# Seven products in place of eight for the gates of the last eight chunks, GpSimd's port in the plan, and new ranks

## The chip, the cores and the metric

One Trainium2 chip, one of its cores. The metric is the time of one execution in microseconds of device time; of several executions the median is given. The profile is of one execution.

## The reference, cut to what matters

Eight sequences of 576 tokens with eight heads go through random-feature attention, and the attended rows, 4,608 tokens of 512 numbers, through a bilinear feed-forward network:

```python
q_p, k_p = (phi(q_s), phi(k_s))            # 128 features a head: exp(x @ omega.T - |x|^2/2 - max)
kv = np.einsum('bhsm,bhsd->bhmd', k_p, v)
num = np.einsum('bhsm,bhmd->bhsd', q_p, kv)
den = np.einsum('bhsm,bhm->bhs', q_p, np.sum(k_p, axis=2))[..., None] + 1e-06
x = num / den                              # to 4608 x 512, heads side by side
a = x @ w1                                 # 512 -> 1024
b = x @ w2                                 # 512 -> 1024
out = ((a * b) @ w3) @ w_out               # 1024 -> 1024 -> 512
```

## The kernel before

The tokens are cut into 36 chunks of 128. Operands of most matmuls are float32 values split into two float16 halves, the value rounded and what is left of it; a product takes three passes (`PASSES`: high by high, high by low, low by high). The weights come as float64 words and are put together at the start; w3 and w_out are multiplied once into one matrix W.

For each chunk, k's features (`k_chunk`: projection `kpj`, maximum, exponential, split) meet v in `kv_batch` when a sequence is complete; q's features (`q_chunk`) are turned by DMA transposes; `q_attend` multiplies them with kv (`nu`), divides, scales by a power of two, splits the result into `xhl` and turns it by a DMA transpose on SP's queue into `xT`, which has three buffers of two chunks each.

`gate` (L1076 to L1124) takes chunks one by one up to chunk 3 and then in pairs. It forms a and b for all 1,024 hidden columns: per pair 8 blocks of hidden columns x 2 (a and b) x 4 blocks of the contraction x 3 passes, with the weights stationary and 256 columns of tokens moving (L1096). ScalarE copies a out of PSUM (L1108), VectorE multiplies b onto it (L1110), GpSimd splits the product into the two halves of `h` (L1116, L1118). `project_out` multiplies h by W, 24 matmuls of 512 columns a chunk (L1137); ScalarE scales the result (L1146) and SP's queue stores it.

No order is written out by hand. Each step is given to `Plan` by `op()` with the engines that could do it and a planned cost on each (`ways`), what it reads and writes, the buffers that it takes, whether it needs the port that VectorE and GpSimd share in the plan (`port`), and a rank. `Plan.order()` plays the program through with these costs: whenever an engine is free it begins the ready step of lowest rank whose buffers are free, and a step that needs the port begins only when no other holds it. The order so found is emitted, and each engine runs its instructions in that order. While TensorE would be idle up to a planned time the plan puts in matmuls with no use (`warm`, L434). A rank is a base (`base(c)`, 15.1 a chunk, less a lead for k and q) plus a number from the table `SHIFT`.

`hi()` (L444 to L447) writes the first half of a split with a per-partition factor; the plan may give it to ScalarE or to GpSimd, with GpSimd's cost `HI_POOL = 0.9` and no claim on the port. `split_raw` does this for q and k (`hlq`, `hlk`; the second half on VectorE at L566), `v_batch` for v (`vhl`), `q_attend` for the attended rows, `part` for the weights. `in_parts` splits the features. The buffers of the features of k (`ek`, six), of the split v (`vhl`, five), of the loaded v (`vraw`, five) and of the split k (`hlk`, one) are used by k's and v's work alone.

## Time and profile before

| | us |
|---|---|
| median of 3 runs | 799.89 (796.57 to 800.54) |
| the profiled execution | 796.71 |
| its span, first to last instruction | 794.5 |
| TensorE busy | 781.3 |
| VectorE, ScalarE, GpSimd busy | 568.9, 398.1, 341.4 |
| mean granted clock of TensorE | 0.997 |

The time contains the span and some 2 us around it. Busy means that an instruction of the engine is under way; matmuls overlap, so their mean duration is longer than their spacing. In the rows PE is TensorE, PEld its weight loads, DVE VectorE, ACT ScalarE, POOL GpSimd, SPq the DMA queue of SyncE; L1096 is a line of the kernel before; "out<-in" are the program's tiles; what stands in brackets or after the bar is idle time before the instruction and what ended it.

### The profile page before, as it was taken

How to read it: one execution, taken by the hardware profiler on the slowest of the kernel's cores; microseconds unless marked ns; L12 is line 12 of the kernel's file. 1: busy time of each engine (PE TensorE's matmuls, PEld its weight loads, DVE VectorE, ACT ScalarE, POOL GpSimd, SP SyncE). 2: the span in 40 equal slices, each digit the busy share in tenths (PEclk: the TensorE clock that was granted, in tenths of full speed). 3: DMA queues.
4: the chain of work that ended last, by engine and by line, in shares of the span. 5: the costliest groups of instructions: out<-in, count | busy, mean ns of one | idle time of the engine just before them, and what ended most of it. 6: DMA issues, size and time to landing. Idle time of an engine off the chain costs nothing.

```text
span 794.5 us, 20125 instructions
## 1 busy us (share of the span) xinstructions
PE 781.3 (98%) x8432; PEld 587.5 (74%) x8437; DVE 568.9 (72%) x1007; ACT 398.1 (50%) x772; POOL 341.4 (43%) x349
## 2 busy tenths in 40 slices
PE   9999899999999999999999999999999999999998
PEld 7856459996678687885978688569585878867674
DVE  6998999995876996777978869779576567544100
ACT  4776346665757594565544555544443434222111
POOL 2323644575663863355544647245235213202121
PEclk9999999999999999999999999999999999999999
DMA  9977665434544524535533743351434434323101
GB/s 349 318 242 214 196 146 135 82 81 95 144 85 106 108 72 96 109 76 145 123 86 67 131 108 94 94 107 42 106 64 78 75 81 105 57 66 69 27 1 54
DMA packets 144491, 88.03 MB, mean 111 GB/s; under 512 B 114576, under 2 KB 122896, under 8 KB 144400
## 3 DMA queue, kind: packets, MB, share of 16 engines
q1 hardware_dynamic: 136384, 74.10, 39.5%
q10 hardware_dynamic: 8016, 12.65, 4.9%
q8 instruction: 66, 1.08, 0.6%
q14 instruction: 25, 0.20, 0.1%
HBM read 49.50 MB, written 9.44 MB: 74 GB/s over the span
## 4 chain that ended last, share of the span: by engine, by line
PE 61%; DVE 7%; ACT 2%; POOL 1%; issue 1%; DMA 1%; SPq 0%; DVEq 0%; ACTq 0%
PE ab L1096 34%; PE o L1137 18%; PE kvp L781 3%; PE qpj L595 2%; PE nu L864 2%; PE kpj L595 2%; DMA qraw<-qT 1%; DVE hlk_k L566 1%; DVE vhl L711 1%; ACT e_k L625 1%; DVE xhl L904 1%; DVE hlq_q L566 1%; DVE e_q L632 0%; DVE nm_q L608 0%; ACT junk L463 0%
## 5 line engine op out<-in xcount | busy, mean ns | idle before, releaser
L1096 PE MATMUL ab<-xT,w12b 128*128 128x256 f16 (+1 forms) x3840 | 391.1, 262 | 1.2 <-DVE asb L1110 1.0
L1096 PEld LDWEIGHTS <-w12b 128*128 128x128 f16 x3840 | 339.3, 98 | 43.9 <-issue 2.4
L1137 PE MATMUL o<-Wb,arena 128*128 128x512 f16 x864 | 193.7, 379 | 0.0
L1137 PEld LDWEIGHTS <-arena 128*128 128x128 f16 x864 | 82.4, 98 | 93.3
L1116 POOL TENSOR_SCALAR arena<-asb 128x512 f16<-128x512 f32 x72 | 52.9, 735 | 227.1 <-DVE asb L1110 184.0
L1110 DVE TENSOR_TENSOR asb<-ab,asb 128x512 f32<-128x512 f32 x72 | 49.5, 687 | 79.0 <-PE ab L1096 68.3
L1118 POOL TENSOR_TENSOR arena<-asb,arena 128x512 f16<-128x512 f32 x72 | 89.8, 1247 | 5.4
L1108 ACT ACTIVATE asb<-ab 128x512 f32<-128x512 f32 x72 | 43.1, 598 | 95.6 <-PE ab L1096 78.0
L1146 ACT ACTIVATE o<-o,oscs 128x512 f32<-128x512 f32 x36 | 24.8, 688 | 58.2 <-PE o L1137 51.9
L646 DVE TENSOR_TENSOR eq<-e_q,eq 128x1024 f16<-128x1024 f32 x29 | 38.7, 1334 | 17.6 <-ACT eq L503 16.1
L608 DVE TENSOR_REDUCE nm_q<-qpj 128x8 f32<-128x1024 f32 x36 | 43.8, 1218 | 7.4 <-PE qpj L595 7.4
L608 DVE TENSOR_REDUCE nm_k<-kpj 128x8 f32<-128x1024 f32 x36 | 43.8, 1219 | 5.0 <-PE kpj L588 3.3
L636 ACT ACTIVATE e_q<-e_q,ln_e,es_q 128x1024 f32<-128x1024 f32 x25 | 31.0, 1239 | 30.3 <-DVE e_q L632 28.0
L446 ACT ACTIVATE xhl<-xs,p2r_x 128x512 f16<-128x512 f32 x29 | 21.1, 727 | 38.0 <-DVE p2r_x L496 37.5
L446 ACT ACTIVATE hlq_q<-qraw,s_q 128x512 f16<-128x512 f32 x23 | 16.6, 720 | 38.4 <-PE qpj L595 37.8
L864 PEld LDWEIGHTS <-eqT 128*128 128x128 f16 (+1 forms) x936 | 29.9, 100 | 6.0 <-issue 1.9
L904 DVE SCALAR_TENSOR_TENSOR xhl<-xs,p2r_x,xhl 128x512 f16<-128x512 f32 x36 | 31.6, 878 | 3.4 <-POOL xhl L447 2.6
L625 ACT ACTIVATE e_k<-kpj,nm_k,es_q 128x128 f32<-128x128 f32 x88 | 32.0, 484 | 4.0 <-DVE nm_k L616 2.6
L646 POOL TENSOR_TENSOR ek<-e_k,ek 128x1024 f16<-128x1024 f32 x14 | 30.7, 2191 | 6.4 <-ACT ek L503 6.0
L1044 PE MATMUL wp<-w12b,arena 128*128 128x512 f32 x64 | 30.2, 628 | 2.7 <-ACT Wb L1055 2.7
L882 DVE TENSOR_SCALAR gd<-nu 128x8 f32<-128x8 f32 x36 | 5.7, 159 | 37.7 <-PE nu L864 37.5
L864 PE MATMUL nu<-kv,eqT 128*128 128x65 f16 (+1 forms) x936 | 32.0, 194 | 0.4 <-DMA eqT<-eq 0.4
(156 smaller groups left out, 1126.3 us busy)
## 6 DMA issues: line engine op xcount, KB each, us to landing
vraw<-v SPq DMA_DIRECT2D x36, 260.0 KB, 3.6
qraw<-qT SPq DMA_DIRECT2D x36, 256.0 KB, 2.8
kraw<-kT SPq DMA_DIRECT2D x36, 256.0 KB, 2.9
out<-o SPq DMA_DIRECT2D x36, 256.0 KB, 2.2
arena<-w3T ACTq DMA_DIRECT2D x6, 1024.0 KB, 5.7
arena<-w ACTq DMA_DIRECT2D x6, 1024.0 KB, 5.9
arena<-wo SPq DMA_DIRECT2D x4, 1024.0 KB, 7.8
arena<-w3T SPq DMA_DIRECT2D x2, 1024.0 KB, 6.0
```

What stands on the lines that cost most here:

```text
L446: return op([(ACT, us, lambda: nc.scalar.mul(dst(), src(), s())), (POOL, pool_us, lambda: nc.gpsimd.tensor_scalar(dst(), src(), s(), None, ...
L608: one(DVE, 1.22, lambda: nc.vector.tensor_reduce(nm.ap, pj(), AX.X, ALU.max, negate=True), r=[pa], w=[nm], new=[nm])
L625: nc.scalar.activation(e.ap[:, h], pj()[:, h], AF.Exp, scale=factor(), bias=nm.ap[:, h : h + 1])
L646: engine(g).tensor_tensor(f16(t.ap)[:, 1], e.ap, f16(t.ap)[:, 0], ALU.subtract)
L864: nc.tensor.matmul(n_[r0:r1, h // 4, h % 4], f16(t.ap)[:, x, place(h), r0:r1], kv_view(kvs[b])[:, y, h], start=n == 0, stop=n == 2,)
L904: lambda: nc.vector.scalar_tensor_tensor(xhl.ap[:, 1], xs.ap, r.ap, xhl.ap[:, 0], ALU.mult, ALU.subtract),
L1096: nc.tensor.matmul(dst, w12[m][i][cc][:, a, r * P : (r + 1) * P], x.ap[:, b, cc, off : off + T], start=j == 0, stop=j == len(mm) - 1,)
L1108: one(ACT, 0.58, lambda: nc.scalar.mul(asb.ap, ab[0].ap, 2.0**-37), r=[(ab[0], k) for k in ks], w=[asb], new=[asb], rank=first)
L1110: one(DVE, 0.69, lambda: nc.vector.tensor_tensor(asb.ap, ab[1].ap, asb.ap, ALU.mult), r=[(ab[1], k) for k in ks], w=[asb], rank=first)
L1116: one(POOL, 0.77, lambda: nc.gpsimd.tensor_scalar(hv()[:, 0], asb.ap, 1.0, 1.0, ALU.mult, ALU.mult), r=[asb], w=[(h, 0)], new=[h], rank=first)
L1118: one(POOL, 1.16, lambda: nc.gpsimd.tensor_tensor(hv()[:, 1], asb.ap, hv()[:, 0], ALU.subtract), r=[asb, (h, 0)], w=[(h, 1)], rank=first, ...
L1137: nc.tensor.matmul(bank.ap, hs[c, f][1]()[:, a], W[f][:, b], start=f0 + i == 0, stop=f0 + 4 == NF and i == len(mm) - 1,)
```

## The change

Three things change together.

*Seven products.* For the last four pairs (chunks 28 to 35) `seven_gate` takes the place of `gate`. For each half i of the hidden columns it looks at a and b of the pair's two chunks as a 2 x 2 block product (w1 and w2 by the two halves of the contraction, the two halves by the two chunks), and forms it from seven block products in place of eight (Strassen's algorithm in Winograd's form). Each product is 4 blocks of hidden columns x 2 of the contraction x 3 passes of 128 columns. Three of the four sums are made in PSUM by writing on into a bank (X and Y, the two banks of a `pa` tile) after ScalarE has copied out what stood there (`snap`), and by additions on VectorE (`plus`). The sums of blocks of the attended rows are made by `seven_parts`, which splits and turns four pieces a pair (X, A, B of full width, C of half width) instead of two; the turned pieces lie in `xT` buffers, two a pair, or for pairs 28 and 32 in one `xT` and the two `kraw` buffers. The sums of blocks of the weights are made once by `sum_weights`, four calls, and lie in all six `ek` and four of the five `vhl` buffers; on the way they use `vraw`. The intermediate copies take `asb`, `hlk` and the last `vhl`.

*The port.* `hi` is left to ScalarE alone; first halves of the features and the rounding steps on GpSimd now claim the port in the plan, with other costs; a few more costs are changed.

*Ranks.* `SHIFT` is replaced throughout (left out here), and k's chunks from 14 on get an earlier rank (`MORE_K`). A second set of constants (`EXACT_B` to `SLOTS`) was put above the first, which stands behind it and overrides it; it has no effect and is left out here. Four more kinds of buffer are given out in program order (`IN_TURN`).

```diff
+MORE_K = 7.0
...
+SEVEN_FROM = 28
+SUM_LEAD = 60.0
...
-    def hi(us, pool_us, dst, src, s, **kw):
-        return op([(ACT, us, lambda: nc.scalar.mul(dst(), src(), s())),
-                   (POOL, pool_us, lambda: nc.gpsimd.tensor_scalar(dst(), src(), s(), None, ALU.mult))][: 1 + (pool_us > 0)], **kw)
+    def hi(us, dst, src, s, **kw):
+        return one(ACT, us, lambda: nc.scalar.mul(dst(), src(), s()), **kw)
...
-        his = [(DVE, 0.7), (ACT, 1.05), (POOL, 1.5)]
...
+        his = [(DVE, 0.7), (ACT, 1.06), (POOL, 1.06)]
...
-           r=[e], w=[(t, 0)], new=new, port=(DVE,))
+           r=[e], w=[(t, 0)], new=new, port=BOTH)
...
+        seven = c >= SEVEN_FROM
+        gd, gr, xs, mx = Buf("gd", str(c)), Buf("gr", str(c)), Buf("vraw" if seven else "xs", f"x{c}"), Buf("mx", str(c))
...
+        pt = pts[c] = Buf("pt", str(c))
...
+        if seven:
+            seven_parts(c, xs, r)
+            return
...
+    def piece(name, src, n, keys, c):
+        xhl, u = Buf("xhl", name), turned[name]
+        def parts():
+            return xhl.ap.rearrange("p x d -> p (x d)")[:, 0 : 2 * n].rearrange("p (x d) -> p x d", x=2)
+        his = ((ACT, 0.72), (POOL, 0.64)) if n == HD else ((ACT, 0.45), (POOL, 0.4))
+        op([(g, us, lambda g=g: move(g, parts()[:, 0], src())) for g, us in his],
+           r=keys, w=[(xhl, 0)], new=[xhl], port=BOTH)
+        los = ((DVE, 0.74), (POOL, 1.16)) if n == HD else ((DVE, 0.42), (POOL, 0.65))
+        op([(g, us, lambda g=g: engine(g).tensor_tensor(parts()[:, 1], src(), parts()[:, 0], ALU.subtract)) for g, us in los],
+           r=keys + [(xhl, 0)], w=[(xhl, 1)], port=BOTH)
+        buf, view = u
+        one(SP, 1.3,
+            lambda: nc.sync.dma_start_transpose(view(), xhl.ap.rearrange("p x d -> p (x d)")[:, 0 : 2 * n]),
+            r=[(xhl, 0), (xhl, 1)], w=[(buf, name)], new=[buf] * (buf.first is None), lat=TURNED)
+    def seven_parts(c, xs, r):
+        x1, h = flat, HD // 2
+        one(ACT, 0.72, lambda: nc.scalar.mul(flat(xs), flat(xs), r.ap), r=[r], w=[xs])
+        normal[c] = xs
+        c0 = c & ~1
+        if c == c0:
+            tags = [["xT"], ["xT"] if c0 % 4 else ["kraw", "kraw"]]
...
+            piece(f"X{c0}", lambda: flat(xs), HD, [xs], c)
+            return
+        X1, X2 = normal[c0], xs
+        ta, tb = Buf("vraw", f"ta{c}"), Buf("vraw", f"tb{c}")
+        adders = ((DVE, 0.42), (POOL, 0.65))
+        def less(dst, a, b, r, w, new=()):
+            op([(g, us, lambda g=g: engine(g).tensor_tensor(dst(), a(), b(), ALU.subtract)) for g, us in adders],
+               r=r, w=w, new=new, port=BOTH)
+        less(lambda: flat(ta)[:, 0:h], lambda: flat(X2)[:, 0:h], lambda: flat(X1)[:, 0:h], [X1, X2], [(ta, 0)], [ta])
+        less(lambda: flat(ta)[:, h:], lambda: flat(X2)[:, h:], lambda: flat(X2)[:, 0:h], [X2], [(ta, 1)])
+        less(lambda: flat(tb)[:, 0:h], lambda: flat(X2)[:, h:], lambda: flat(ta)[:, 0:h], [X2, (ta, 0)], [(tb, 0)], [tb])
+        less(lambda: flat(tb)[:, h:], lambda: flat(X1)[:, h:], lambda: flat(tb)[:, 0:h], [X1, (tb, 0)], [(tb, 1)])
+        piece(f"A{c0}", lambda: flat(ta), HD, [(ta, 0), (ta, 1)], c)
+        piece(f"B{c0}", lambda: flat(tb), HD, [(tb, 0), (tb, 1)], c)
+        piece(f"C{c0}", lambda: flat(X2)[:, h:], h, [X2], c)
...
-            for g, us in ((DVE, 0.69), (POOL, 1.4))], w=[mag], port=(DVE,))
+            for g, us in ((DVE, 0.69), (POOL, 1.06))], w=[mag], port=BOTH)
...
-        one(POOL, 0.77, lambda: nc.gpsimd.tensor_scalar(hv()[:, 0], asb.ap, 1.0, 1.0, ALU.mult, ALU.mult),
-            r=[asb], w=[(h, 0)], new=[h], rank=first)
+        op([(g, us, lambda g=g: move(g, hv()[:, 0], asb.ap)) for g, us in ((POOL, 0.64), (ACT, 0.74))],
+           r=[asb], w=[(h, 0)], new=[h], rank=first, port=BOTH)
...
+    sums = {}
+    def sum_weights(i, cc):
+        def pair(n, c):
+            return w12[n][i][c], ("b", i, n * NC + c)
+        both = ((DVE, 0.7), (POOL, 1.16))
+        def two(name, a, b, sign, keys):
+            t = Buf("vraw", name)
+            op([(g, us, lambda g=g: engine(g).tensor_tensor(flat(t), a(), b(), sign)) for g, us in both],
+               r=keys, w=[t], new=[t], port=BOTH)
+            return t
+        def whole(n, c):
+            w, key = pair(n, c)
+            return two(f"r{n}{i}{c}", lambda: w[:, 0], lambda: w[:, 1], ALU.add, [key])
+        def keep(name, a, b, sign, last=False):
+            op([(g, us, lambda g=g: engine(g).tensor_tensor(flat(a), flat(a), flat(b), sign)) for g, us in both],
+               r=[b], w=[a], port=BOTH)
...
+        def split(k, t):
+            place = sums[k, i, cc] = seats.pop(0)
+            buf, view = place
...
+            op([(g, us, lambda g=g: move(g, view()[:, 0], flat(t))) for g, us in ((ACT, 0.72), (POOL, 0.64))],
+               r=[t], w=[key], new=fresh, port=BOTH)
+            op([(g, us, lambda g=g: engine(g).tensor_tensor(view()[:, 1], flat(t), view()[:, 0], ALU.subtract)) for g, us in both],
+               r=[t], w=[key], port=BOTH)
+            sums[k, i, cc] = view, key
+        a21, a11 = whole(1, cc), whole(0, cc)
+        s3 = two(f"s3_{i}{cc}", lambda: flat(a11), lambda: flat(a21), ALU.subtract, [a11, a21])
+        split(3, s3)
+        a22 = whole(1, cc + 2)
+        keep("s1", a21, a22, ALU.add)
+        split(1, a21)
+        keep("s2", a21, a11, ALU.subtract)
+        split(2, a21)
+        a12 = whole(0, cc + 2)
+        keep("s4", a12, a21, ALU.subtract)
+        split(4, a12)
...
+    def seven_gate(c0, i, rank):
+        xy, w = Buf("pa", f"xy_{c0}_{i}"), Buf("pm", f"w_{c0}_{i}")
+        def plain(n, c):
+            return lambda: w12[n][i][c], ("b", i, n * NC + c)
+        def summed(k, c):
+            return sums[k, i, c]
+        def block(name, k):
+            buf, view = turned[f"{name}{c0}"]
+            m = 2 if name == "C" else 4
+            return (lambda c, b: view()[:, b * m + 2 * k + c]), (buf, f"{name}{c0}")
+        everything = [block(n, 0)[1] for n in "XABC"] + [sums[k, i, c][1] for k in range(1, 5) for c in range(2)]
+        def product(dst, key, ws, x, start, new=()):
+            xv, xkey = x
+            def go():
+                for f in range(4):
+                    mm = [(c, a, b) for c in range(2) for a, b in PASSES]
+                    for j, (c, a, b) in enumerate(mm):
+                        nc.tensor.matmul(
+                            dst()[:, f * P : (f + 1) * P], ws[c][0]()[:, a, f * P : (f + 1) * P], xv(c, b),
+                            start=start and f == 0 and j == 0, stop=j == len(mm) - 1, skip_group_check=True,
+                        )
+            one(PE, 1.3, go, r=[x_[1] for x_ in ws] + [xkey] + (everything if xy in new else []), w=[key], new=new, rank=rank)
+        X, Y, Wd = (lambda: xy.ap[:, 0]), (lambda: xy.ap[:, 1]), (lambda: w.ap)
+        kx, ky, kw = (xy, 0), (xy, 1), (w, 0)
+        first = rank - 1000
+        s1, u2, u3 = Buf("asb", f"s1_{c0}_{i}"), Buf("hlk", f"u2_{c0}_{i}"), Buf("vhl", f"u3_{c0}_{i}")
+        def f32(b):
+            return b.ap if b.tag == "asb" else b.words[:, 0:512]
+        def snap(t, scale):
+            one(ACT, 0.58, lambda: nc.scalar.mul(f32(t), X(), scale), r=[kx], w=[t], new=[t], rank=first)
+        def plus(t, dst, key, scale):
+            if scale == 1.0:
+                one(DVE, 0.69, lambda: nc.vector.tensor_tensor(f32(t), dst(), f32(t), ALU.add), r=[key], w=[t], rank=first)
+            else:
+                one(DVE, 0.69, lambda: nc.vector.scalar_tensor_tensor(f32(t), dst(), scale, f32(t), ALU.mult, ALU.add),
+                    r=[key], w=[t], rank=first)
+        def out_parts(c, t):
+            h = Buf("h", f"{c}_{i}")
+            def hv():
+                return h.ap.rearrange("p (x i) -> p x i", x=2)
+            op([(g, us, lambda g=g: move(g, hv()[:, 0], f32(t))) for g, us in ((POOL, 0.64), (ACT, 0.74))],
+               r=[t], w=[(h, 0)], new=[h], rank=first, port=BOTH)
+            op([(g, us, lambda g=g: engine(g).tensor_tensor(hv()[:, 1], f32(t), hv()[:, 0], ALU.subtract)) for g, us in ((POOL, 1.16), (DVE, 0.74))],
+               r=[t, (h, 0)], w=[(h, 1)], rank=first, port=BOTH)
+            for f in range(4):
+                hs[c, 4 * i + f] = (
+                    h, lambda f=f: h.ap.rearrange("p (x f s) -> p x f s", x=2, f=4)[:, :, f]
+                )
+        product(X, kx, [plain(0, 0), plain(0, 1)], block("X", 0), True, [xy])
+        snap(s1, 2.0**-37)
+        product(Wd, kw, [plain(0, 2), plain(0, 3)], block("X", 1), True, [w])
+        plus(s1, Wd, kw, 2.0**-37)
+        product(X, kx, [(sums[2, i, c]) for c in range(2)], block("B", 0), False)
+        snap(u2, 2.0**-37)
+        product(Y, ky, [(sums[1, i, c]) for c in range(2)], block("A", 0), True)
+        product(X, kx, [(sums[3, i, c]) for c in range(2)], block("A", 1), False)
+        snap(u3, 1.0)
+        plus(u3, Y, ky, 1.0)
+        product(X, kx, [plain(1, 2), plain(1, 3)], block("B", 1), False)
+        one(DVE, 0.69, lambda: nc.vector.tensor_tensor(s1.ap, X(), s1.ap, ALU.mult), r=[kx], w=[s1], rank=first)
+        out_parts(c0, s1)
+        product(Y, ky, [(sums[4, i, c]) for c in range(2)], block("C", 0), False)
+        plus(u2, Y, ky, 2.0**-37)
+        op([(g, us, lambda g=g: engine(g).tensor_tensor(f32(u2), f32(u2), f32(u3), ALU.mult)) for g, us in ((DVE, 0.7), (POOL, 1.16))],
+           r=[u3], w=[u2], rank=first, port=BOTH)
+        out_parts(c0 + 1, u2)
...
-    def ranks(early, lead):
+    def ranks(early, lead, more=0.0):
         r = list(early)
         while len(r) < NCH:
-            r.append(max(base(len(r)) - lead, r[-1] + 4))
+            r.append(max(base(len(r)) - lead - more * max(0, len(r) - 14), r[-1] + 4))
         return r.__getitem__
...
+    for i in range(2):
+        for cc in range(2):
+            plan.at("sum", 2 * i + cc, base(SEVEN_FROM) - SUM_LEAD + 8 * (2 * i + cc))
+            sum_weights(i, cc)
...
     for c0, n in groups:
+        if c0 >= SEVEN_FROM:
+            for i in range(2):
+                seven_gate(c0, i, plan.at("gate", 2 * c0 + i, base(c0) + 2 * i))
+            continue
         for u in range(2 * n):
```

## Rows read from the trace of the kernel before

**Rows 1.** The page: busy us, share of the span, instructions of each engine.

```profile
PE 781.3 (98%) x8432; PEld 587.5 (74%) x8437; DVE 568.9 (72%) x1007; ACT 398.1 (50%) x772; POOL 341.4 (43%) x349
```

**Rows 2.** Stretches of the span: length, then busy us (instructions) of each engine, clock, DMA.

```profile
core 0: us, PE busy (x) PEld busy (x) DVE busy (x) ACT busy (x) POOL busy (x), PEclk, DMA share, GB/s
0.00:100.00 100.00, 95.57 (x650) 64.92 (x652) 85.27 (x121) 60.66 (x142) 37.68 (x55) 0.98 0.81 262
100.00:180.00 80.00, 78.97 (x1088) 66.39 (x1091) 74.26 (x133) 49.69 (x111) 44.64 (x38) 1.00 0.48 110
...
743.00:794.50 51.50, 47.77 (x364) 35.38 (x362) 4.15 (x6) 6.33 (x10) 10.64 (x12) 0.99 0.06 21
...
180.00:640.00 460.00, 455.95 (x5345) 344.48 (x5343) 351.49 (x641) 248.17 (x465) 223.34 (x222) 1.00 0.44 96
640.00:743.00 103.00, 103.00 (x993) 76.36 (x992) 53.70 (x108) 33.23 (x45) 25.09 (x25) 1.00 0.35 75
```

**Rows 3.** TensorE by line and form: count, busy us, mean ns of one.

```profile
L1096 PE MATMUL ab<-xT,w12b 128*128 128x128 f16 x768 | 44.7, 219 | 0.2
...
L434 PE MATMUL warm<-ones 128*128 128x256 bf16 x105 | 14.5, 295 | 1.0 <-DVE unscaled L357 1.0
...
L1096 PEld LDWEIGHTS <-w12b 128*128 128x128 f16 x3840 | 339.3, 98 | 43.9 <-issue 2.4
```

**Rows 4.** Timeline of TensorE, four places: start us, length us, merged count.

```profile
146.26 10.88 PE L1096 MATMUL ab<-xT,w12b 128*128 128x128 f16 x192
...
620.80 1.99 PE L781 MATMUL kvp<-vhl,ek 128*128 128x65 f16 x60
...
743.63 25.05 PE L1096 MATMUL ab<-xT,w12b 128*128 128x256 f16 x228
...
780.25 10.52 PE L1137 MATMUL o<-Wb,arena 128*128 128x512 f16 x48
```

**Rows 5.** ScalarE by line and form.

```profile
L1108 ACT ACTIVATE asb<-ab 128x512 f32<-128x512 f32 x72 | 43.1, 598 | 95.6 <-PE ab L1096 78.0 <-POOL arena L1118 7.0 <-PE norm_q L469 5.7
...
L446 ACT ACTIVATE hlq_q<-qraw,s_q 128x512 f16<-128x512 f32 x23 | 16.6, 720 | 38.4 <-PE qpj L595 37.8 <-DVE s_q L483 0.4
```

**Rows 6.** GpSimd by line and form: three of the seven groups of L447.

```profile
L447 POOL TENSOR_SCALAR vhl<-vraw,sv_v 128x512 f16<-128x512 f32 x13 | 24.1, 1864 | 4.0 <-DVE pv L695 4.0
...
L447 POOL TENSOR_SCALAR w12b<-w12b,ws 128x512 f16<-128x512 f32 x7 | 15.8, 2254 | 8.5 <-DVE w12b L1027 7.6 <-DVE ws L1019 0.9
...
L447 POOL TENSOR_SCALAR hlq_q<-qraw,s_q 128x512 f16<-128x512 f32 x7 | 10.9, 1562 | 9.1 <-ACT hlk_k L446 3.5 <-PE norm_v L469 3.4 <-issue 1.7
```

**Rows 7.** VectorE by line and form, whole span; the last row from 560 us on.

```profile
L1110 DVE TENSOR_TENSOR asb<-ab,asb 128x512 f32<-128x512 f32 x72 | 49.5, 687 | 79.0 <-PE ab L1096 68.3 <-PE norm_q L469 10.2 <-ACT vhl L446 0.2
...
L566 DVE SCALAR_TENSOR_TENSOR hlk_k<-kraw,s_q,hlk_k 128x512 f16<-128x512 f32 x25 | 28.9, 1158 | 2.7 <-ACT hlk_k L446 2.0 <-POOL hlk_k L447 0.7
...
L566 DVE SCALAR_TENSOR_TENSOR hlq_q<-qraw,s_q,hlq_q 128x512 f16<-128x512 f32 x9 | 6.7, 743 | 0.0
```

**Rows 8.** Timeline of TensorE, VectorE and GpSimd, 490 to 499 us.

```profile
497.12 0.73 PE L595 MATMUL kpj<-om,hlk_k 64*128 64x128 f16 x20 [1.39 <-DVE hlk_k L566]
498.38 1.47 PE L1096 MATMUL ab<-xT,w12b 128*128 128x256 f16 x12 [0.53 <-DVE asb L1110]
...
493.27 3.79 DVE L566 SCALAR_TENSOR_TENSOR hlk_k<-kraw,s_q,hlk_k 128x512 f16<-128x512 f32 x1
...
487.56 6.12 POOL L447 TENSOR_SCALAR vhl<-vraw,sv_v 128x512 f16<-128x512 f32 x3
...
494.24 2.27 POOL L1118 TENSOR_TENSOR arena<-asb,arena 128x512 f16<-128x512 f32 x2
```

**Rows 9.** Stretch from 646.4 us, line L1096 alone: busy us (instructions) of PE, PEld.

```profile
646.40:794.50 148.10, 85.07 (x766) 74.06 (x763) 1.00 0.23 54
```

**Rows 10.** Tile xhl, 640 to 760 us: ns min/median/max.

```profile
L922 SPq DMA_TRANSPOSE xT<-xhl x7: 1233/1238/1310, 639.1 to 737.1; - x7
...
DMA to landing us min/median/max: 3.0/3.0/3.2
```

More of the change, by code (lines that the diff above doesn't have):

```diff
@@ new lines @@
+    "v": [0.0, 0.0, -19.8129, -69.8506, 203.3918, 88.777, 52.5064, 103.654],
+}
+HI_POOL = 1.7
+EXACT_B = 2
+EXACT_K = (0, 5, 9, 14, 18)[EXACT_B]
+FAST_K = 9
+FAST_Q = 4
+EXACT_Q = 1
+PROJECT_K = 9
+AHEAD = 5
+PROJECT_Q = 4
+KEYED_K = 9
+KEYED_Q = 5
+ORDER = "ooooWW11a22bWWWWWW11a22bS"
+WRANK = [4.0 * i for i in range(25)]
+KRANK = [4.0, 10.0, 16.0, 22.0, 28.0, 110.0, 115.0, 120.0, 125.0, 129.0, 133.0, 137.0]
+QRANK = [40.0, 70.0, 80.0, 90.0, 124.0, 142.0]
+GRANK = 100.0
+BASE = 110.0
+PERIOD = 18.5
@@ L277 @@
+LEAD_Q = 60.0
+LEAD_K = 145.0
+GROUPS = [(0, 1), (1, 1), (2, 1), (3, 1)]
+GROUP = 2
+ARENA = 21
+RAW64_BUFS = 3
+SLOTS = {
+    "kraw": 2, "qraw": 2, "hlk": 1, "hlq": 1, "e": 2, "ek": 6, "vraw": 5, "vhl": 5, "kv": 3, "eq": 1, "eqT": 2,
[3 rows of a table added]
+}
 EXACT_B = 2
@@ L618, in bias @@
                 )
-            op([(g, us, lambda g=g: bias(g)) for g, us in [(DVE, 0.2), (POOL, 0.35)][: 1 + exact]],
-               r=key, w=[nm], port=(DVE,))
+            op([(g, us, lambda g=g: bias(g)) for g, us in [(DVE, 0.2), (POOL, 0.24)][: 1 + exact]],
+               r=key, w=[nm], port=BOTH)
             def exps():
@@ L766, in low @@
             nc.vector.tensor_tensor(u[:, 1, :, z], f.ap[:, :, z], u[:, 0, :, z], ALU.subtract)
-        one(DVE, 1.1, low, r=[(f, 0), (f, 1), s, (t, 0)], w=[(t, 1)], port=BOTH)
+        one(DVE, 1.85, low, r=[(f, 0), (f, 1), s, (t, 0)], w=[(t, 1)], port=BOTH)
         kvs[b] = t
@@ L891, in quotient @@
             )
-        one(DVE, 1.13, quotient, r=[nu], w=[gd, gr, xs], new=[gd, gr, xs])
+        one(DVE, 1.13, quotient, r=[nu], w=[gd, gr, xs], new=[gd, gr] if seven else [gd, gr, xs])
         one(DVE, 0.68,
-            lambda: nc.vector.tensor_reduce(mx.ap, xs.ap, AX.X, ALU.max, apply_absolute_value=True),
+            lambda: nc.vector.tensor_reduce(mx.ap, flat(xs), AX.X, ALU.max, apply_absolute_value=True),
             r=[xs], w=[mx], new=[mx])
@@ L900, in q_attend, with back @@
         )
+        pt = pts[c] = Buf("pt", str(c))
+        def back():
+            for b, r0, r1 in owners:
+                k = unscaled if exact else pv[b].ap
+                nc.vector.tensor_scalar(pt.ap[r0:r1], p.ap.bitcast(F32)[r0:r1], k[r0:r1], None, ALU.mult)
+        one(DVE, 0.2 * len(owners), back, r=[p] + ([] if exact else [pv[b] for b, _, _ in owners]), w=[pt], new=[pt])
+        if seven:
+            seven_parts(c, xs, r)
+            return
         xhl = Buf("xhl", str(c))
-        hi(0.72, HI_POOL, lambda: xhl.ap[:, 0], lambda: xs.ap, lambda: r.ap, r=[xs, r], w=[(xhl, 0)], new=[xhl])
+        hi(0.72, lambda: xhl.ap[:, 0], lambda: xs.ap, lambda: r.ap, r=[xs, r], w=[(xhl, 0)], new=[xhl])
         one(DVE, 0.74,
@@ L907, in q_attend @@
             r=[xs, r, (xhl, 0)], w=[(xhl, 1)], port=BOTH)
-        pt = pts[c] = Buf("pt", str(c))
-        def back():
-            for b, r0, r1 in owners:
-                k = unscaled if exact else pv[b].ap
-                nc.vector.tensor_scalar(pt.ap[r0:r1], p.ap.bitcast(F32)[r0:r1], k[r0:r1], None, ALU.mult)
-        one(DVE, 0.16 * len(owners), back, r=[p] + ([] if exact else [pv[b] for b, _, _ in owners]), w=[pt], new=[pt])
         mc, off = c * P // TOK, c * P % TOK
@@ new lines, in seat, with view @@
+    def seat(buf, k):
+        def view():
+            t = buf.ap.rearrange("p a b -> p (a b)").bitcast(F16) if buf.tag == "ek" else buf.ap.rearrange("p a h e -> p (a h e)")
+            return t[:, k * 1024 : k * 1024 + 1024].rearrange("p (x f) -> p x f", x=2)
+        return buf, view
+    seats = []
+    for b in [Buf("ek", f"sum{n}") for n in range(6)]:
+        seats += [seat(b, 0), seat(b, 1)]
+    seats += [seat(Buf("vhl", f"sum{n}"), 0) for n in range(4)]
+    def seven_gate(c0, i, rank):
[64 more added lines that the diff above has]
+        out_parts(c0 + 1, u2)
```

58 lines of the change are left out of this document (39 added, 19 removed), and 31 rows, old and new, of tables (SHIFT, SLOTS).

## The prediction

> **What bounds the kernel now.** I read the page's busy table first [rows 1]: TensorE is busy for 781.3 of 794.5 us, VectorE for 568.9, ScalarE for 398.1, GpSimd for 341.4. Busy shares can hide slow matmuls, so next the stretches [rows 2]: from 180 us to the last matmul TensorE is without work for about 4 us in all (460.00 - 455.95 up to 640, nothing from 640 to 743), at a granted clock of 1.00. Before 180 us it lacks 5.5 us (100.00 - 95.57 and 80.00 - 78.97), and 105 warm-up matmuls, 14.5 us of them, fill time in which it had nothing useful to do [rows 3]. After the last matmul some 3.7 us pass (last slice: 51.50 - 47.77). So the length of the kernel is the sum of its matmuls plus about 28 us, and an edit counts by what it does to that sum and to those waits.
>
> VectorE is the engine that could take over. It is busy 351.49 of 460 us (76%) between 180 and 640 us, and 74.26 of 80 (93%) between 100 and 180, where TensorE was nevertheless kept at 78.97 of 80 [rows 2]. The chain of waits shows the same: through the middle it runs partly over VectorE and GpSimd.
>
> **The seven products.** A pair of chunks now takes 192 matmuls of 256 columns in its gates. With seven products for each half of the hidden columns it takes 2 x 7 x 4 x 2 x 3 = 336 matmuls of 128 columns: 43,008 columns where there were 49,152, but 1.75 times as many instructions and weight loads. The page's mean durations overlap, so I take the spacing in unbroken runs [rows 4]: 228 matmuls of 256 columns in 25.05 us are 109.9 ns each; 192 of 128 columns, in the first chunks, in 10.88 us are 56.7 ns each, although each of these too has its own weight load of 98 ns [rows 3]. Per pair 192 x 109.9 = 21.10 us become 336 x 56.7 = 19.04. Four pairs: 84.4 us become 76.2, a gain of **8.2 us**.
>
> A rule speaks against this. The Trainium skill (TensorE: Matmul & The Clock Gate, section Back-to-back issue gap) gives about 81 ns for each matmul of 128 columns in a sustained stream where every one has its weight load. By it 1,344 of them would take an estimated 108.9 us, 24.5 more than the gates take now, and the kernel would come out near 821. The run of 192 at 56.7 ns [rows 4] disagrees, and I go by the run.
>
> **Waits inside a seven-product gate.** The sums X and Y stay open in PSUM and are copied out in between, so TensorE may write X again only when ScalarE's copy is done. Of the three copies of X, two are covered by another product of 24 x 56.7 = 1.36 us; the third has none behind it in the gate. A copy takes 598 ns [rows 5]; with its two handovers I take 1.0 us. If another gate or an output product (12 matmuls, a quarter of 10.52 us [rows 4]) stands in the order there, it costs nothing; if nothing does, 8 gates x 1.0 = 8 us. The order is worked out by a planner that puts other ready work there, and the trace shows outputs between gates right up to the end. I take the middle, **+4 us**, bounds 0 and 8.
>
> **GpSimd and its port.** The plan counts 0.9 us for GpSimd's scaling by a per-partition factor. The trace has 52 of them, in seven groups with means from 1,562 to 2,254 ns, 95.9 us together [rows 6] (three of the groups stand there). The change gives all to ScalarE, where the same step takes 720 ns [rows 5]: 52 x 0.72 = 37 us more there. With 16 copies for the sums (12 us) and some 3.7 us more in each of the four pairs (two more copies out of PSUM, two scalings, one and a half first halves) it comes to 398 + 37 + 12 + 15 = 462 us, under 60% of the span: hidden. What they cost now is seen on VectorE: there the second half of k's split takes 1,158 ns on average where the same step for q takes 743 late in the kernel, when GpSimd is quiet [rows 7]. At 493.27 us one takes 3.79 us, while GpSimd, held up by 6.12 us for three scalings, runs two subtractions for 2.27 us; TensorE waits 1.39 us for it and 0.53 us for the step behind it [rows 8]. A plan that keeps the two engines apart should avoid much of that. Bounds: nothing, and all 4 us of TensorE's idle time after 180 us. I take **-4 us**, since the largest wait there, 1.9 us of these 4, comes from just this.
>
> **Sums of weights.** Four calls, each with 8 sums, 4 splits: 48 operations of 512 columns for VectorE or GpSimd, 16 copies. The nearest row is VectorE's product at 687 ns [rows 7]: 33 us if VectorE takes them all. They live in the buffers of the k features and of v, so all work on k must be over first. Now the last k product runs at 620.80 us [rows 4], and 768 gate matmuls, as many as the last four pairs have, run from about 646 [rows 9] (766 counted). The changed ranks pull k forward. Between 180 and 640 VectorE then has up to 351.5 + 33 = 384.5 us of work, 84% of 460; without part of its waits for the port (k's split alone has 25 x 0.41 = 10 us of them) nearer 80%. It has been seen at 93% with TensorE fed, so I cost this at **nothing**; without that cover it is the rival below.
>
> **The end.** After the last product of a gate four steps follow (addition, multiplication and two for the halves; with VectorE's 687 ns for the first two and some 0.7 and 1.2 us for the others about 3.3 us). The 48 output matmuls that end the kernel now, 10.52 us [rows 4], cover them, as chunk 34's 24 need nothing of chunk 35's. Gates of one pair share the single `hlk` buffer: the second wants it 3 x 1.36 = 4.1 us after it begins, when the first has just freed it.
>
> **The rest of the last chunks.** Per pair VectorE gets six more full-width steps, four half ones and about 1.5 splits, some 6.6 us by the 687 ns row, 26 us in all, where it is busy 53.70 of 103 us and then 4.15 of 51.5 [rows 2]: hidden. Each pair sends four pieces through the one buffer for split attention rows instead of two. A piece takes about 0.72 + 0.74 us for its halves and 3.0 us from issue to landing [rows 5, 7, 10], so the pieces of a pair need some 18 us, less than the 19.0 us of gates of the pair before them: hidden, unless the buffers for turned rows (three, of which a pair may now take two) come free late. The 1.5 extra transposes per pair hold SP's queue for about 1.24 us each [rows 10], behind which the next loads of q and the outputs stand; near the end there are few.
>
> **Ranks anew** reorder the whole kernel. Before 180 us up to 20 us (5.5 idle, 14.5 of warm-up) could in principle be won, or as much lost; DMA is busy 81% there in the first 100 us, which leaves little to win. I take nothing, bounds -8 and +8.
>
> **The sum.** -8.2 + 4 - 4 = -8.2 us on the profiled execution's 796.71: **788.5 us**. The median of the runs shown, 799.89, lies 3.2 us above that execution (which is close to the lowest run, 796.57), so a median may lie up to 3.2 higher; I say **790**.
>
> **The rivals.**
> - *As forecast*, 783 to 795.9: chance 0.55.
> - *Better*: the new order also wins 5 us or more of the first 180 us (8 would give 780.5). For it: 20 us without useful work there. Against: the DMA share. Chance 0.14.
> - *The gain is given back in waits*: third copies uncovered (+8) or the turned pieces late. If a pair waits for its 18 us of pieces behind only one chunk's output (10.5 us for two chunks, so 5.3 for one), two pairs lose 2 x 12.7 = 25 at worst; a third of it, 8, makes 796.7. For it: one buffer, four pieces. Against: outputs left over as filler. 796 to 803, chance 0.16.
> - *VectorE becomes the bound before pair 28* (the side of slower). The 384.5 us must fit in the 460 us that TensorE needs. If VectorE can be kept only 80% busy there, they take 480.6, 20.6 more: 796.7 - 8.2 + 20.6 = 809. At its present 76.4% they would take 503, and the kernel 832. It decides from 384.5 / (460 + 8.2) = 82% downward. For it: VectorE and its partners are on the chain now. Against: 93% between 100 and 180. Chance 0.13.
> - *Weight loads don't hide*: each matmul of 128 columns then waits its 98 ns, 1,344 x 98 = 131.7 us instead of 84.4, and the kernel takes 844. The run of 192 speaks against it; chance 0.02. The Trainium skill's figure in the section named above is a milder form of this.
>
> **Range and chances.** Leaving out the lower half of *better*, the weight loads and most of *VectorE* gives 780 to 802. About 0.5% is what a measurement of this kernel can tell; from 799.89 that is 795.9 and 803.9. The first two cases are faster: 0.69, and 0.01 of the third; its rest, 0.15, is the same; the last two, 0.15, slower.
>
> **What would show it.** Gates at a spacing of 56 to 57 ns in the last four pairs, 336 per pair; no GpSimd scaling over 1 us by a factor; k's second half near 0.75 us; k's last product well before the sums of weights; TensorE still 98% busy. The prediction is wrong if TensorE shows gaps before the first seven-product gate with VectorE as releaser, or between products with ScalarE's copy as releaser, or if the first 180 us come out several us longer or shorter.

## The result, and the profile after

The changed kernel takes 785.40 us (median of four runs, 783.11 to 786.60); the kernel before took 799.45 in the same four rounds (796.57 to 800.54). The ratio is 0.9823, 95% interval 0.9808 to 0.9837: about 14 us faster. The forecast was 790, range 780 to 802, so the direction and the range were right, and the gain came out larger than the sum. The profiled execution takes 783.11 us (span 781.1), 13.6 less than the 796.71 that the sum started from.

The first views, busy time by engine from the page, and the stretches of the span with the columns of [rows 2]:

```profile
PE 771.6 (99%) x9025; PEld 587.3 (75%) x9025; DVE 595.3 (76%) x1092; ACT 464.4 (59%) x899; POOL 235.5 (30%) x273
```

```profile
core 0: us, PE busy (x) PEld busy (x) DVE busy (x) ACT busy (x) POOL busy (x), PEclk, DMA share, GB/s
0.00:100.00 100.00, 97.47 (x624) 65.09 (x625) 84.33 (x124) 66.58 (x153) 15.01 (x42) 1.00 0.87 269
100.00:180.00 80.00, 79.63 (x1111) 64.36 (x1110) 72.89 (x152) 58.83 (x126) 20.43 (x18) 1.00 0.47 118
180.00:640.00 460.00, 459.61 (x5575) 355.57 (x5574) 372.97 (x696) 291.49 (x550) 174.14 (x188) 1.00 0.46 98
640.00:743.00 103.00, 100.74 (x1404) 80.58 (x1403) 56.95 (x112) 38.67 (x61) 24.35 (x24) 1.00 0.37 68
743.00:781.10 38.10, 34.16 (x317) 21.69 (x315) 8.16 (x12) 8.84 (x14) 1.61 (x1) 0.98 0.09 35
```

Against [rows 1, 2] the reader is to see three things. TensorE's time without work before 180 us falls from 5.46 to 2.90 us, and its granted clock in the first 100 us is 1.00 instead of 0.98 (0.97 in its repeat, see the last section). Between 180 and 640 us the time without work falls from 4.05 to 0.39, although VectorE has 21.5 us more to do there. From 640 to 743, where nothing was missing, 2.26 us now are. ScalarE comes to 464.4 us (462 were forecast) and GpSimd to 235.5, down 106.

The new matmuls, by line and form (count, busy us, mean ns of one, idle before); these are three of the seven groups of L1317, which hold 1,344 in all, and the warm-up:

```profile
L1317 PE MATMUL xy<-xT,ek_sum 128*128 128x128 f16 x432 | 33.3, 219 | 0.0
...
L473 PE MATMUL warm<-ones 128*128 128x256 bf16 x117 | 16.0, 293 | 1.1 <-DVE unscaled L392 1.1
...
L1317 PE MATMUL w<-xT,w12b 128*128 128x128 f16 x192 | 11.9, 219 | 0.1
L1317 PE MATMUL xy<-kraw_x,ek_sum 128*128 128x128 f16 x144 | 11.1, 219 | 1.4 <-ACT asb_s L1333 1.4
```

The means of 219 ns overlap; the spacing is read from the timeline. TensorE near 652 us, and under it ScalarE in the same stretch (start, length, in brackets the idle time before and what ended it):

```profile
651.57 1.51 PE L1317 MATMUL xy<-xT,w12b 128*128 128x128 f16 x24
652.92 1.50 PE L1317 MATMUL xy<-xT,ek_sum 128*128 128x128 f16 x24
655.11 1.50 PE L1317 MATMUL xy<-kraw_x,ek_sum 128*128 128x128 f16 x24 [0.69 <-ACT asb_s L1333]
```

```profile
654.46 0.60 ACT L1333 ACTIVATE asb_s<-xy 128x512 f32<-128x512 f32 x1 [2.06 <-PE xy L1317]
```

From 651.57 to 652.92 are 24 matmuls in 1.35 us, 56 ns each. Over all 1,344 the median from one start to the next is 56 ns, so the gates are worth 75.3 us (76.2 forecast, 84.4 before). These three products show the new wait. The first writes X and ends at 653.08. The second (A by a sum of weights) writes Y, the other bank of the same `pa` tile, and ends at 654.42. Only then does ScalarE, idle since 652.40, copy X, from 654.46 to 655.06, and TensorE goes on with X at 655.11. So the copy begins when the product that could have covered it is over. Near 687 us the product behind the one into X is W, which has a tile of its own, and there the copy begins beside it; first TensorE, then ScalarE:

```profile
686.39 1.50 PE L1317 MATMUL xy<-xT,w12b 128*128 128x128 f16 x24
687.97 1.50 PE L1317 MATMUL w<-xT,w12b 128*128 128x128 f16 x24
```

```profile
687.99 0.60 ACT L1333 ACTIVATE asb_s<-xy 128x512 f32<-128x512 f32 x1 [0.19 <-PE xy L1317]
```

The same holds the other way round: a product into X begins only when VectorE's addition from Y (`plus`) is over, at 661.41.

```profile
660.72 0.69 DVE L1337 TENSOR_TENSOR vhl_u<-xy,vhl_u 128x512 f32<-128x512 f32 x1 [0.15 <-ACT vhl_u L1333]
```

```profile
661.46 1.50 PE L1317 MATMUL xy<-kraw_x,w12b 128*128 128x128 f16 x24
```

It looks as if these waits go by the tile and not by the bank. That is a reading of the trace: no run gave X and Y tiles of their own. VectorE's and GpSimd's steps, by line and form over the whole span:

```profile
L604 DVE SCALAR_TENSOR_TENSOR hlk_k<-kraw,s_q,hlk_k 128x512 f16<-128x512 f32 x25 | 21.1, 844 | 0.4 <-ACT hlk_k L485 0.4
```

```profile
L545 POOL TENSOR_SCALAR ek_sum<-vraw_r 128x512 f16<-128x512 f32 x3 | 1.8, 616 | 5.9 <-PE kvp L819 5.9
```

The second half of k's split falls from 1,158 ns [rows 7] to 844, with 25 instances in both. GpSimd's row is of a TENSOR_SCALAR of the same shape that takes constants, 616 ns; with a factor per partition none of the groups was below 1,562 [rows 6].

The last product for k comes some 50 us earlier: it starts at 571.2 us, where it was 620.80 [rows 4]. The sums of weights run from 516 to 619 us, and the first seven-product gate begins at 630.69. Stretches from 560 to 620 us, same columns:

```profile
560.00:580.00 20.00, 20.00 (x294) 15.78 (x291) 17.25 (x26) 11.04 (x16) 12.12 (x12) 1.00 0.43 80
580.00:600.00 20.00, 20.00 (x218) 17.51 (x217) 19.22 (x29) 10.82 (x17) 11.18 (x9) 1.00 0.19 41
600.00:620.00 20.00, 20.00 (x174) 13.46 (x173) 17.48 (x35) 8.47 (x16) 6.41 (x5) 1.00 0.22 54
```

TensorE is never without work, but VectorE is at 90% (53.95 of 60): the sums are covered, with little to spare.

One wait of the kernel before was not among the rows of the prediction. Its timeline near 94 us, and the stretch behind it:

```profile
93.57 8.83 PE L1044 MATMUL wp<-w12b,arena 128*128 128x512 f32 x16 [2.65 <-ACT Wb L1055]
```

```profile
93.50:97.00 3.50, 3.43 (x4) 1.39 (x5) 3.33 (x7) 1.78 (x4) 2.54 (x2) 0.53 0.77 275
```

ScalarE's copy stood behind a chain of scalings of the weights that alternates between VectorE and GpSimd, and a GpSimd one took up to 2.98 us. TensorE waited 2.65 us, and then its granted clock was 0.53 for 3.5 us, near the lower of its two levels (1.2 of 2.4 GHz): the matmuls there took some 850 ns instead of 429, together 1.7 us more. The changed kernel has neither at this place.

**The clock of each run.** This matters for reading small differences. The mean granted clock is known for every run. It is 0.991 to 0.998 in 35 later runs of the kernel before, and 0.995 to 0.999 in the four of the changed one. (1 - clock) x span estimates the time lost; rounding makes it uncertain by 0.4 us. Times less that estimate are called "at full clock" below, and only beside the measured ones.

### The profile page after: what moved, and what is told of

It reads as the page before. It is cut to its first block, busy times and chain, and to the rows that moved or that the text cites. A ratio compares the mean times of both kernels' runs of the same rounds, so it can differ in the third digit from the quotient of the medians.

```text
span 781.1 us, 21441 instructions
## 1 busy us (share of the span) xinstructions
PE 771.6 (99%) x9025; PEld 587.3 (75%) x9025; DVE 595.3 (76%) x1092; ACT 464.4 (59%) x899; POOL 235.5 (30%) x273
## 4 chain that ended last, share of the span: by engine, by line
PE 88%; issue 5%; DVE 2%; DMA 2%; ACT 1%; POOLq 0%; POOL 0%; ACTq 0%; DVEq 0%
PE ab L1204 37%; PE o L1387 21%; PE wp L1152 7%; PE xy L1317 5%; PE nu L904 3%; PE kvp L819 3%; PE qpj L633 3%; DMA kraw<-kT 2%; PE kpj L633 2%; PE kvp L766 2%; PE kpj L626 1%; PE warm L473 1%; PE w L1317 1%; PE qpj L626 1%; PE l L1110 0%
## 5 line engine op out<-in xcount | busy, mean ns | idle before, releaser
L1204 PE MATMUL ab<-xT,w12b 128*128 128x256 f16 (+1 forms) x3072 | 305.2, 259 | 0.1
L1204 PEld LDWEIGHTS <-w12b 128*128 128x128 f16 x3072 | 264.5, 98 | 31.8 <-issue 0.8
L1226 POOL TENSOR_TENSOR arena<-asb,arena 128x512 f16<-128x512 f32 x56 | 73.5, 1312 | 86.7 <-ACT arena L541 82.5
L1218 DVE TENSOR_TENSOR asb<-ab,asb 128x512 f32<-128x512 f32 x56 | 38.5, 688 | 22.8 <-PE ab L1204 16.6
L646 DVE TENSOR_REDUCE nm_k<-kpj 128x8 f32<-128x1024 f32 x36 | 43.7, 1219 | 14.2 <-PE kpj L633 10.8
L541 ACT CAST arena<-asb 128x512 f16<-128x512 f32 x39 | 24.0, 614 | 29.3 <-DVE asb L1218 29.2
L545 POOL TENSOR_SCALAR arena<-asb 128x512 f16<-128x512 f32 x17 | 11.5, 676 | 97.8 <-DVE asb L1218 76.0
L1317 PEld LDWEIGHTS <-ek_sum 128*128 128x128 f16 x576 | 35.5, 98 | 3.0 <-issue 1.7
L1317 PEld LDWEIGHTS <-w12b 128*128 128x128 f16 x576 | 33.3, 98 | 3.0 <-issue 1.3
L1056 ACT ACTIVATE arena<-arena 128x1024 f32<-128x1024 f32 x20 | 23.0, 1160 | 18.8 <-DMA arena<-w 7.5
L1317 PE MATMUL xy<-xT,ek_sum 128*128 128x128 f16 x432 | 33.3, 219 | 0.0
L1062 POOL TENSOR_SCALAR arena<-arena 128x1024 f32<-128x1024 f32 x11 | 11.9, 1082 | 66.1 <-ACT arena L1056 65.9
```

Of the source, the lines that this page charges most:

```text
L646: one(DVE, 1.22, lambda: nc.vector.tensor_reduce(nm.ap, pj(), AX.X, ALU.max, negate=True), r=[pa], w=[nm], new=[nm])
L1204: nc.tensor.matmul(dst, w12[m][i][cc][:, a, r * P : (r + 1) * P], x.ap[:, b, cc, off : off + T], start=j == 0, stop=j == len(mm) - 1,)
L1218: one(DVE, 0.69, lambda: nc.vector.tensor_tensor(asb.ap, ab[1].ap, asb.ap, ALU.mult), r=[(ab[1], k) for k in ks], w=[asb], rank=first)
L1226: one(POOL, 1.16, lambda: nc.gpsimd.tensor_tensor(hv()[:, 1], asb.ap, hv()[:, 0], ALU.subtract), r=[asb, (h, 0)], w=[(h, 1)], rank=first, ...
L1317: nc.tensor.matmul(dst()[:, f * P : (f + 1) * P], ws[c][0]()[:, a, f * P : (f + 1) * P], xv(c, b), start=start and f == 0 and j == 0, stop ...
```

## The experiments

The surplus over the forecast called for a cause. **Theory 1:** GpSimd's scalings cost more than the 4 us that I gave them, since they hold the port also where TensorE shows no wait of its own; the seven products bring the forecast net of 4. **Theory 2, the rival:** the new ranks and order bring it, or the products bring their full 8 with no waits. Medians stand against the kernel before, run beside each group: 798.77 us for the first four runs, 797.22 for the next four, 798.57 for the last four.

**b_const.** The kernel before in its own order; GpSimd's 52 scalings use constant factors, which leaves the scaling out:

```diff
-nc.gpsimd.tensor_scalar(dst(), src(), s(), None, ALU.mult)
+nc.gpsimd.tensor_scalar(dst(), src(), 1.0, 1.0, ALU.mult, ALU.mult)
```

> The kernel before in its own order; GpSimd's 52 scalings multiply by the constants 1.0 and 1.0 instead of a per-partition factor, so the scaling of those halves is left out. Theory 1: what the change won beyond my sum comes from these scalings, which hold VectorE up, before 180 us too. Then they take some 0.65 to 0.75 us each like the splits of h on GpSimd, about 37 us instead of 95.9, the second half of k's split falls from 1,158 to about 800 ns, the wait near 90 us goes, and the time is 5 to 8 us shorter, 791 to 794. Theory 2: it comes from the new order; then the scalings get shorter but the time stays within 1.5 us of before, 798 to 801.

791.6 us, ratio 0.9908 (0.9886 to 0.9930): 7.2 faster with nothing moved. By line and form on GpSimd and VectorE, and TensorE's timeline at the wait of 94 us:

```profile
L447 POOL TENSOR_SCALAR hlq_q<-qraw 128x512 f16<-128x512 f32 x7 | 4.3, 618 | 20.1 <-PE qpj L595 14.2 <-ACT hlk_k L446 3.5 <-issue 2.3
...
L447 POOL TENSOR_SCALAR w12b<-w12b 128x512 f16<-128x512 f32 x7 | 7.3, 1049 | 11.0 <-DVE w12b L1027 11.0
```

```profile
L566 DVE SCALAR_TENSOR_TENSOR hlk_k<-kraw,s_q,hlk_k 128x512 f16<-128x512 f32 x25 | 22.3, 892 | 2.0 <-ACT hlk_k L446 2.0
```

```profile
93.32 7.13 PE L1044 MATMUL wp<-w12b,arena 128*128 128x512 f32 x16 [1.41 <-ACT Wb L1055]
```

The same timeline at the wait of [rows 8], and the stretch from 180 us on:

```profile
494.20 0.73 PE L595 MATMUL kpj<-om,hlk_k 64*128 64x128 f16 x20 [0.44 <-DVE hlk_k L566]
```

```profile
180.00:640.00 460.00, 457.81 (x5367) 346.29 (x5365) 343.66 (x640) 250.19 (x466) 183.00 (x221) 1.00 0.43 97
```

The same seven scalings of q take 618 ns instead of 1,562 [rows 6], and k's second half 892 instead of 1,158 [rows 7]. TensorE's wait for it at 494 us is 0.44 us instead of 1.39 [rows 8]. All six runs have a clock of 1.000. So of the 7.2 about 2.8 are clock, and I put the other 4.4 down to waits (791.6 against 796.0 at full clock). The two profiled executions show about half of that: TensorE's time without work falls from 13.2 to 10.8 us, and 1.9 of this lies between 180 and 640 us. The Trainium skill (SBUF — State Buffer, section SBUF: two separate sides) says that a GpSimd operation and certain VectorE operations lock each other out of a shared port for a whole instruction; VectorE's shorter times here agree with it.

**b_const_w.** The same with only the 12 scalings of weights.

> The kernel before in its own order; only the 12 scalings of weights on GpSimd (7 of w1 and w2, 5 of W) use the constants 1.0 and 1.0, so the scaling of those halves is left out. If the wait of TensorE near 90 us and the slow clock behind it (2.65 and some 1.7 us) come from these, 2 to 4 of the 7 us that all 52 brought are seen, about 795. If the gain comes from the 40 of q, k, v and the attended rows, it stays within 1 us of before.

795.51, ratio 0.9963 (0.9952 to 0.9974): 3.1 faster, of which about 1 is clock; the 12 scalings start between 80 and 182 us. The wait, on TensorE's timeline:

```profile
93.07 7.13 PE L1047 MATMUL wp<-w12b,arena 128*128 128x512 f32 x16 [1.59 <-ACT Wb L1058]
```

**b_hiact.** The kernel before with its ranks; first halves on ScalarE alone, order planned anew: `[: 1 + (pool_us > 0)], **kw)` becomes `[:1], **kw)`.

> The kernel before with its own ranks and costs; first halves go to ScalarE alone, so the order is planned anew with that one choice less. Theory 1 (scalings): 3 to 7 us shorter, 792 to 796, with no wait over 1 us on TensorE near 90 us. Theory 2 (new ranks): within 3 us of before, 796 to 802, either way.

806.56, ratio 1.0094 (1.0066 to 1.0123): a miss, 7.8 slower. TensorE's largest waits (releaser, us in total, times, longest):

```profile
PE ab L1096 <- ACT ek L503: 3.7, 1, 3.7
PE ab L1096 <- DMA xT<-xhl: 3.3, 1, 3.3
```

Taking GpSimd off the scalings is no gain by itself: the order planned from the old ranks has two long waits ahead of gates.

**a_no7.** The changed kernel with eight products everywhere and no sums of weights; port and ranks as changed: `SEVEN_FROM = 36`.

> The changed kernel with the eight products kept for the last eight chunks and no sums of weights; port and ranks as changed. If the seven products are worth their matmul time less the new waits between them (8.4 - 4.1 us), this takes 4 to 5 us longer than the changed kernel, about 790. If the whole gain hung on them, about 797 to 799. If they brought nothing, about 785.

789.83, ratio 0.9891 (0.9868 to 0.9915): 8.9 faster than before and 4.4 slower than the changed kernel (785.4, measured at another time; by the ratios of its two measurements the difference is 2.8 to 5.4). The stretches:

```profile
180.00:640.00 460.00, 459.42 (x5608) 360.83 (x5607) 356.74 (x679) 286.32 (x543) 153.64 (x172) 1.00 0.47 99
640.00:743.00 103.00, 103.00 (x930) 79.18 (x929) 35.07 (x68) 25.19 (x37) 18.22 (x15) 1.00 0.21 42
```

The gain between 180 and 640 us is there without the products, and nothing is missing after 640. Its clock (median 0.997) is that of the kernel before, so here the 8.9 are not clock (8.5 at full clock).

**a_snap.** The changed kernel in its order; the three copies read an SBUF tile instead of X, so they no longer hold X:

```diff
-nc.scalar.mul(f32(t), X(), scale)
+nc.scalar.mul(f32(t), Wb[:, NF], scale)
```

> The changed kernel in its own order; ScalarE's three copies of X per gate read a finished tile in SBUF instead of X, so the values of the gates of the last eight chunks are wrong and TensorE need not wait for the copies. If the new idle time of TensorE after 640 us (2.3 us, and some 8 times 0.23 us between products) is waits for these copies, the time falls by 2.5 to 4 us, to about 782. If it comes from the switches between products, it falls by less than 1 us.

782.05, ratio 0.9788 (0.9764 to 0.9813): 3.4 faster than the changed kernel's 785.4 (by the ratios again 2.8 to 5.4). Its stretch at the end:

```profile
640.00:743.00 103.00, 102.50 (x1425) 81.73 (x1418) 58.78 (x116) 39.24 (x61) 24.38 (x24) 1.00 0.39 73
```

**a_wafter.** The third sum (W) may run only behind X, to see whether the waits for the first copy go: `+ ([kx] if key is kw else [])` in the product's reads.

> The changed kernel with one more dependency in the plan: the product W of a gate comes after the first product X, so that it stands between X and its next turn. The order of the last chunks is planned anew. If the two waits of 0.7 us for ScalarE's copy come from W having been moved ahead, they go and the time falls by 1 to 1.5 us, to about 784.5. If other waits take their place, it stays or rises.

787.55, ratio 0.9855 (0.9833 to 0.9876): a miss, no gain. The waits named for copies, the same columns as above:

```profile
PE xy L1317 <- DVE hlk_u L1339: 1.8, 2, 1.0
...
PE xy L1317 <- DVE vhl_u L1337: 0.9, 1, 0.9
...
PE xy L1317 <- ACT hlk_u L1333: 0.7, 1, 0.7
PE xy L1317 <- ACT vhl_u L1333: 0.7, 1, 0.7
```

The wait for the first copy is gone. Now the second and third copies are waited for, and above all VectorE's additions behind them.

**a_seven32.** Seven products for the last two pairs only: `SEVEN_FROM = 32`.

> The changed kernel with seven products for the last two pairs only. The net gain of the seven products was 4.4 us for four pairs; if it is a sum over pairs, half of it is left and the time is about 788. If the sums of weights or the last pair alone decide, it is nearer 785.5 or 790.

786.1, ratio 0.9857 (0.9837 to 0.9876): by the medians no different from four pairs, and not the 788 of a sum over pairs. At full clock a_no7, this one and the changed kernel are 787.5, 785.3 and 782.2 (783.0 in its repeat). By that estimate each two pairs would be worth about half; the measured times do not show it.

**a_sum2.** The changed kernel; 36 of the 48 additions and subtractions of the sums issued twice in a row: `for _ in range(2)` behind them.

> The changed kernel in its own order; 36 of the 48 additions and subtractions of the sums of weights are given twice in a row, with the same result, some 25 us more for VectorE and GpSimd before the first seven-product gate. If VectorE has the room that my estimate gave it (81% busy there, 93% seen elsewhere), the time stays within 2 us of the changed kernel. If VectorE is at its bound there, a good part of the 25 us comes out, 8 us or more.

804.88, ratio 1.0088 (1.0072 to 1.0105): 18.7 slower than the changed kernel beside it, for 24 us more of VectorE and 25 of GpSimd.

**a_sum0.** The opposite: 32 of the operations on 32 of their 512 columns, the splits reading a block of the weights instead of the sums.

> The changed kernel in its own order; 32 of the 48 additions and subtractions of the sums of weights work on 32 of their 512 columns, and the splits behind them take a weight block in place of the sum, so the sums are wrong. If the sums as they stand cost nothing, as I forecast (TensorE is busy without a gap from 540 to 640 us), the time stays within 1.5 us of the changed kernel. If VectorE is the bound there already, it falls by 4 to 12 us.

785.47, ratio 0.9839 (0.9811 to 0.9868). The stretch from 540 to 640 us in three kernels, first a_sum2, then the changed kernel (its repeat), then a_sum0:

```profile
540.00:640.00 100.00, 86.18 (x982) 68.97 (x980) 89.16 (x126) 39.32 (x63) 53.13 (x42) 1.00 0.27 51
```

```profile
540.00:640.00 100.00, 100.00 (x1112) 77.86 (x1112) 78.52 (x139) 49.84 (x77) 42.34 (x36) 1.00 0.35 70
```

```profile
540.00:640.00 100.00, 100.00 (x1122) 77.89 (x1121) 63.57 (x138) 49.17 (x78) 32.85 (x36) 1.00 0.34 70
```

As they stand the sums cost nothing: shrinking them takes VectorE from 78.5 to 63.6 us, and TensorE had 100 of 100 already. Doubled, they break the cover: TensorE is without work for 13.8 of these 100 us.

**a_hipool17.** The changed kernel with GpSimd allowed for first halves again, planned at 1.7 us and without the claim on the port; order anew:

```diff
-return one(ACT, us, lambda: nc.scalar.mul(dst(), src(), s()), **kw)
+return op([(ACT, us, lambda: nc.scalar.mul(dst(), src(), s())),
+           (POOL, 1.7, lambda: nc.gpsimd.tensor_scalar(dst(), src(), s(), None, ALU.mult))], **kw)
```

> The changed kernel with GpSimd again allowed for the first halves with a factor, at a planned cost of 1.7 and without a claim on the port. The order is planned anew. Theory 1 (these scalings are what held the kernel up): it loses 4 to 8 us if GpSimd gets some 20 or more of them, 789 to 794, with VectorE's second halves back near 1 us. Theory 2 (the new ranks won it): within 2 us of the changed kernel.

805.65, ratio 1.0098 (1.0082 to 1.0114): 19.5 slower than the changed kernel beside it, more than either theory said. GpSimd and TensorE by line and form:

```profile
L486 POOL TENSOR_SCALAR xhl<-xs_x,p2r_x 128x512 f16<-128x512 f32 x13 | 24.5, 1887 | 18.5 <-DVE p2r_x L535 12.8 <-issue 5.1 <-DVE pt L946 0.6
```

```profile
L473 PE MATMUL warm<-ones 128*128 128x256 bf16 x223 | 28.1, 283 | 1.1 <-DVE unscaled L392 1.0
```

59 scalings went back to GpSimd (106 us). The visible price is 12 us more of warm-up matmuls, 28.1 instead of 16.0, that is useful work not ready, and waits. Here the port and the order changed together, so the run says that this order with these engines is bad, not what a scaling costs.

**a_cost.** A product of a gate planned at 1.34 instead of 1.30 us, which gives another order: does the time hang on one lucky order?

> The changed kernel with the planned cost of one product at 1.34 in place of 1.3, what the trace shows for 24 matmuls; nothing else. If the ranks fit only the order they were found with, planning anew costs several us, 788 to 795. If the plan is robust, within 1.5 us of the changed kernel.

785.72, ratio 0.9851 (0.9833 to 0.9868): no difference. **after_again** is the changed kernel once more, beside the second four:

> The changed kernel once more, on the chip of the runs beside it: 785 to 786, and the base for them.

786.19, ratio 0.9856 (0.9842 to 0.9869).

No run has the old ranks in the changed kernel, or the new ones in the old, or the port claims and the other changed costs one by one. The parts within port and ranks stay unseparated.

## Why the prediction was right, and where it was off

**The seven products: right.** Net -4.4 us by a_no7 (2.8 to 5.4 by the ratios), where -8.2 + 4 = -4.2 was forecast. The spacing is 56 ns (56.7 forecast), so the rival of weight loads falls. The rule of 81 ns per matmul (the Trainium skill, TensorE: Matmul & The Clock Gate, section Back-to-back issue gap) would have given about 821 us, by the estimate in the prediction. The trace disagrees: the median is 56, and none of the spacings in these gates lies between 69 and 287 ns.

**Waits inside a gate: right in size, wrong in place.** +4 was forecast; a_snap gives 3.4. In the trace nine products start late by the spacing of 56 ns, by 3.4 us together. I expected the first two copies of a gate to be covered by a product and the third to be bare. But the two waits of 0.7 us in the idle column (0.85 and 0.91 by the spacing) are for the first copy (asb_s). The planner had moved the product W, which was to cover it, ahead, and the product into Y that stood there instead did not cover it: the copy began only behind it. The other seven are 0.23 us each, on VectorE's addition behind a copy, six of them behind the third; the idle column shows 0.07 of each. So the cover as I put it is what failed here, and that 3.4 comes so near the middle of 0 and 8 is in part luck. Gaps with ScalarE's copy as releaser were named as a sign that the prediction is wrong, and two are there. a_wafter shows that moving W merely moves the wait.

**GpSimd and its port: right for the waits, too narrow a bound.** Forecast -4 with at most 4, all from TensorE's idle time after 180 us. The factor alone is worth 7.2 us in the old order: by the medians 4.4 of waits and 2.8 of clock. In the stretch that the forecast meant, TensorE's idle time went from 4.05 us to 2.19 in b_const, and to 0.58 in a_no7, which has the port claims and the new order too. So the -4 fits all three together, and the scalings alone are about half of it. k's second half came to 844 ns, where about 750 was named. 3.1 of the 7.2 come from scalings that start between 80 and 182 us (b_const_w), a stretch where the step as I put it did not look. But the changed kernel does not keep the clock's share: its median clock (0.996) is no better than the old one's, as it loses it at another place (last section).

**Ranks anew: this step failed**, "I take nothing", with bounds of 8 either way. GpSimd's scalings, port claims and ranks together bring 8.9 (a_no7). At full clock that is 8.5, and b_const's waits are 4.4; so some 4 us remain for the order, with its port claims. The profiled executions say the same: less the 1.7 us that a slow stretch cost the kernel before (at 94 us) and a_no7 (between 38 and 44 us, at 0.72), a_no7 is 6.4 us faster and b_const 2.2. That figure is a difference of two runs in different orders, and the causes in it were not separated. By it each theory is about half right, which is argued and not shown. The DMA share, by which I held the first 180 us to be filled, did not stop 2.6 us of TensorE's idle time there from going, at a DMA share of 0.87 instead of 0.81; the warm-up took 1.5 back (14.5 to 16.0). That ranks and choice of engine belong together fits b_hiact (7.8 slower than before) and a_hipool17 (19.5 slower than the changed kernel, and slower than before): in both the choice of engine changed and the ranks did not.

**Sums of weights at no cost: right, but the reason was too generous.** VectorE had 373.0 us between 180 and 640 (81% of 460; 80 to 84% were forecast), and a_sum0 shows a cost of nothing. The rival (VectorE as bound before pair 28) fell, yet it was near. I argued from 93% seen between 100 and 180 us; in the stretch where the sums fall, VectorE's 90% was about the limit, and a_sum2's 24 us came out as 18.7 (GpSimd's 25 more may have had a part in that; no run separates the two).

**The end and the rest of the last chunks: right.** From the last matmul to the end are 3.7 us, as before; VectorE is at 56.95 of 103 us.
